# Two weight sums on VectorE, state additions ahead of the recombination, and the last product in banks of its own, in a fused attention and gated feed-forward kernel

## The chip, the cores and the metric

One core of one Trainium2 chip. The metric is the device time of the whole program in microseconds (us). The kernel before was given with a median of 321.29 us (three runs, 321.08 to 322.13). The span of the profiled execution is about 1.7 us shorter than the time of the same run, so spans and times are not mixed below.

## The reference, cut to what matters

```python
# q, k, v: (8 batches, 8 heads, 576 positions, 64); w_in (512, 2048); w_out (2048, 512)
scores = q @ k^T / 8                      # per batch and head
ret    = scores * Dmat                    # gamma_h ** (i - j) where i >= j, else 0
x      = (ret @ v) as (4608 tokens, 512)
h      = x @ w_in
out    = (h * cos(h)) @ w_out             # (4608, 512), float32
```

## The kernel before

The tokens go in ten blocks `n` of 512, 256, 256 and seven times 512. TensorE does all products. In each block it first multiplies by `w_in` (the rows `PE ... h<-xT,w_in_sb` of the profile), ScalarE takes the cosine, VectorE makes the gated activations `gT`, and then TensorE multiplies by `w_out`. Attention for later blocks (scores, states, output: `sc`, `st`, `ov`) is laid between the products. GpSimd (POOL) prepares token groups of 128: it scales queries and keys and casts values (`qks`, `vb`) once their loads have landed.

From block 3 on (`S7 = 3`) the last multiplication is done in 2x2 quarters with seven products instead of eight. That needs sums of weight quarters (`w_sums`), once, and sums of activation quarters (`g_sum`, tiles `gs`; the prediction calls them operand sums), in every block. The seven products are then added to and subtracted from each other on VectorE to give the four output quarters; this is called the recombination. A product's matmuls add up in an accumulator (`ps`), which lies in one or more banks of the memory that TensorE writes to. Products are made in the order 3, 4, 5, 2, 1, 7, 6. Products 3 and 4 need weight sums 3 and 4, which overwrite quarters of `w_out_sb` in place, so they cannot be made before block 2 has read the weights.

```python
def w_sums(x, e0, e1):
    # ... a, b, op_ by x; for x in (3, 4) the result overwrites quarter a of w_out_sb
    (nc.gpsimd if x in (3, 4) else nc.vector).tensor_tensor(
        out=w_sum[x][:, e0:e1], in0=w_quarter(*a)[:, e0:e1], in1=w_quarter(*b)[:, e0:e1], op=op_)

def g_sum(n, x, e0, e1):
    # ...
    i = (nc.vector if x == 5 or (n, x) == (S7, 1) else nc.gpsimd).tensor_tensor(
        out=tiles["gs", n, x][:, e0:e1], in0=i0, in1=i1, op=op_)

def sums_after(n, i):                      # after w_in multiplication number i of block n
    if n == S7:
        if i == 0:
            w_sums(3, 0, E2)
            w_sums(4, 0, E2)
        if i == 6:
            g_sum(n, 5, 0, 4)
            g_sum(n, 2, 0, 4)
        elif i == 7:
            for x, e in ((5, 4), (2, 4), (1, 0), (7, 0), (6, 0)):
                g_sum(n, x, e, E2)
    elif i in (3, 7):
        for x in (5, 2, 1, 7, 6):
            g_sum(n, x, i - 3, i + 1)

def product(n, x):                         # 16 matmuls of 256 columns
    if x in (3, 4, 1, 7):
        ps = psum.tile([P, 2, N2], F32, tag={3: "n", 4: "st", 1: "n", 7: "st"}[x], name="o")
    # ... else it accumulates: 5 on 3, 2 on 4, 6 on 1
    for e in range(E2):
        for j in range(2):                 # two row blocks
            nc.tensor.matmul(ps[:, j], lhsT=lhs[:, e, j * P : (j + 1) * P], rhs=rhs[:, e, :], ...)

def mm2_seven(n, at):
    # ...
    for x in (3, 4, 5, 2, 1, 7, 6):
        if x in at:
            at[x](*[both] * (x == 5))      # attention work laid before product x
        # ...
        product(n, x)
        # x == 2: c21 = copy of the accumulator (ScalarE), then
        nc.vector.tensor_tensor(out=u22, in0=u22, in1=tiles["o", 4], op=ALU.subtract)
        # x == 1, 7, 6: additions into u11, u11, u22; each result is stored and feed() called,
        # which queues the preparation, transposes and loads of later token groups

def unit7(g, more=True, then=lambda: None):
    copy = states([g + 1, g + 2], "b")()   # state products, then the state additions (VectorE)
    then()
    attn_out([g, g + 1], "m", nc.scalar.copy)
    if more:
        scores2(g + 2)                     # banks "a" and "b"
    copy(nc.scalar.copy)
```

## Time and profile before

Three numbers matter: 15.2 us in which TensorE waits once for the weight sums; about 31 us for each later block, which TensorE fills to 98%; and the last block, where TensorE waits for GpSimd's sums.

The second part of the page shows the span in 40 slices of 8 us, each digit a busy share in tenths; PEclk is the granted clock of TensorE.

```profile
PE   8899999999993079999999999999999999999984
POOL 2760176545434899959995999599969944970793
PEclk9999999999998559999999999999999999999999
```

The hole in TensorE's row, the only one, is at 96 to 120 us, with the clock at half. GpSimd is not full before it. The table of TensorE's waits names what ended them (who waited, for whom: total us, how often, the longest):

```profile
PE o L441 <- POOL w_out_sb L374: 15.2, 1, 15.2
PE sc L181 <- DVE s L263: 2.4, 4, 0.7
PE o L441 <- POOL gs L396: 1.7, 4, 1.3
```

GpSimd's timeline shows why the sums were late (start, duration, engine, line, operation, number; in brackets the idle time before it and what ended that):

```profile
103.41 1.04 POOL L138 TENSOR_TENSOR qks<-fq,gq 128x512 bf16<-128x512 f32 x1 [4.28 <-DMA fq<-in_q_dram]
107.07 1.04 POOL L138 TENSOR_TENSOR qks<-fq,gq 128x512 bf16<-128x512 f32 x1 [0.61 <-DMA fq<-in_q_dram]
109.26 0.61 POOL L145 CAST vb<-fv 128x512 bf16<-128x512 f32 x1
109.83 8.06 POOL L374 TENSOR_TENSOR w_out_sb<-w_out_sb 128x2048 bf16<-128x2048 bf16 x2
117.84 12.28 POOL L396 TENSOR_TENSOR gs<-gT 128x1024 bf16<-128x1024 bf16 x4
```

The weight sums stand behind the preparation of token groups 16 and 17, which waits for loads, and the activation sums stand behind the weight sums. TensorE's timeline of the same stretch:

```profile
113.92 3.57 PE L441 MATMUL o<-w_out_sb,gT 128*128 128x256 bf16 x16 [15.20 <-POOL w_out_sb L374]
124.75 0.40 PE L181 MATMUL sc<-qkT 64*128 64x128 bf16 x8 [0.57 <-DVE s L263]
130.17 3.67 PE L441 MATMUL o<-ws,gs 128*128 128x256 bf16 x32
133.68 13.98 PE L321 MATMUL h<-xT,w_in_sb 128*128 128x512 bf16 x62
```

Product 3 runs 113.92 to 117.5 at half clock (3.57 us for 16 matmuls; 1.8 at full clock), products 7 and 6 are the row at 130.17, and block 4 begins at 133.68. The wait on `DVE s` is a score product that needs the bank of the state products back. In block 6 one sees the order that causes it:

```profile
219.34 0.58 ACT L483 COPY ot<-o 128x512 f32<-128x512 f32 x1 [1.16 <-DMA fk<-in_k_dram]
219.96 0.69 DVE L484 TENSOR_TENSOR ot<-ot,o 128x512 f32<-128x512 f32 x1 [1.06 <-ACT ot L483]
220.56 0.42 DVE L261 COPY s<-st 128x256 f32<-128x256 f32 x1
221.02 0.42 DVE L263 TENSOR_TENSOR s<-st,s 128x256 f32<-128x256 f32 x1
221.59 0.40 PE L181 MATMUL sc<-qkT 64*128 64x128 bf16 x8 [0.68 <-DVE s L263]
```

VectorE waits 1.06 us for a ScalarE copy in order to recombine, and only then makes the state additions for which TensorE waits. The end of the span:

```profile
297.83 17.16 POOL L396 TENSOR_TENSOR gs<-gT 128x1024 bf16<-128x1024 bf16 x8 [12.14 <-DVE gs L396]
315.05 1.05 PE L441 MATMUL o<-ws,gs 128*128 128x256 bf16 x8 [0.16 <-POOL gs L396]
316.13 0.69 DVE L492 TENSOR_TENSOR ot<-o,ot 128x512 f32<-128x512 f32 x1 [1.39 <-PE o L441]
```

GpSimd makes eight sums in a row to 315.0 us, and the last eight matmuls start when it ends. After the last addition (316.82) 3.2 us pass to the end of the span at 320.0.

### The profile page before, as it was taken

What the parts mean: (1) busy time and instruction counts of PE and PEld (TensorE: products, weight loads), DVE (VectorE), ACT (ScalarE), POOL (GpSimd) and SP (SyncE); (2) the same over time, 40 slices, a digit from 0 to 9 for tenths busy, and PEclk for the clock granted to TensorE, in tenths of its full rate; (3) what the DMA queues carried; (4) which work ended last, traced back from release to release, by engine and by line L of the source; (5) the groups of instructions that cost most, each with busy time, mean ns of one, the idle gap of its engine ahead of it and who ended that gap; (6) DMA issues with size and microseconds to landing.
All of it is one profiled execution on the core that took longest, in us unless ns stands there. A gap on an engine that the chain in (4) does not pass through costs nothing.

```text
span 320.0 us, 6597 instructions
## 1 busy us (share of the span) xinstructions
PE 292.7 (91%) x2724; PEld 200.7 (63%) x2745; DVE 200.1 (63%) x238; ACT 139.3 (44%) x176; POOL 222.8 (70%) x181
## 2 busy tenths in 40 slices
PE   8899999999993079999999999999999999999984
PEld 3578458575882057746874676477647754884563
DVE  5767745747687026378767784778387747835832
ACT  2666225333463004364346472645265536525610
POOL 2760176545434899959995999599969944970793
PEclk9999999999998559999999999999999999999999
DMA  8999999999999994999969953997670250021012
GB/s 213 209 211 206 199 236 221 183 219 239 177 195 213 236 209 113 195 219 206 226 156 244 196 127 66 201 228 168 135 163 2 68 131 2 0 87 46 2 58 73
DMA packets 154109, 50.23 MB, mean 157 GB/s; under 512 B 140768, under 2 KB 153056, under 8 KB 154080
## 3 DMA queue, kind: packets, MB, share of 16 engines
q1 hardware_dynamic: 149856, 45.63, 72.6%
q0 software_dynamic: 4224, 4.19, 7.9%
q8 instruction: 21, 0.34, 0.5%
q14 instruction: 8, 0.07, 0.1%
HBM read 36.70 MB, written 9.44 MB: 144 GB/s over the span
## 4 chain that ended last, share of the span: by engine, by line
PE 68%; POOL 8%; SPq 8%; DMA 8%; DVE 3%; issue 3%; ACT 1%; POOLq 1%
PE h L321 32%; PE o L441 22%; DMA fk<-in_k_dram 8%; SPq L113 6%; PE o L338 6%; POOL gs L396 5%; PE sc L181 3%; PE ov L294 2%; PE ov L281 2%; POOL w_out_sb L374 1%; POOL qks L139 1%; SPq L154 1%; ACT cosh L329 1%; PE st L240 1%; DVE s L263 1%
## 5 line engine op out<-in xcount | busy, mean ns | idle before, releaser
L396 POOL TENSOR_TENSOR gs<-gT 128x1024 bf16<-128x1024 bf16 (+1 forms) x52 | 115.3, 2254 | 34.3 <-DVE gs L396 34.3
L321 PE MATMUL h<-xT,w_in_sb 128*128 128x512 bf16 (+2 forms) x820 | 126.8, 313 | 0.8
L330 DVE TENSOR_TENSOR gT<-h,cosh 128x1024 bf16<-128x1024 f32 x72 | 88.1, 1224 | 46.5 <-ACT cosh L329 46.3
L329 ACT ACTIVATE cosh<-h,half_pi 128x1024 f32<-128x1024 f32 x72 | 80.2, 1113 | 73.5 <-PE h L321 73.5
L321 PEld LDWEIGHTS <-w_in_sb 128*128 128x128 bf16 x832 | 75.9, 98 | 49.0 <-issue 0.4
L138 POOL TENSOR_TENSOR qks<-fq,gq 128x512 bf16<-128x512 f32 x32 | 34.0, 1061 | 43.5 <-DMA fq<-in_q_dram 43.3
L441 PEld LDWEIGHTS <-gs 128*128 128x128 bf16 x560 | 53.5, 98 | 10.1 <-POOL gs L396 2.9
L190 DVE TENSOR_TENSOR ret<-sc,tri 128x1024 bf16<-128x1024 f32 x32 | 38.0, 1219 | 18.5 <-PE sc L181 18.3
L139 POOL TENSOR_TENSOR qks<-fk,gk 128x512 bf16<-128x512 f32 x35 | 37.0, 1059 | 10.3 <-DMA fk<-in_k_dram 9.6
L441 PE MATMUL o<-w_out_sb,gT 128*128 128x256 bf16 x224 | 28.0, 286 | 15.2 <-POOL w_out_sb L374 15.2
L441 PE MATMUL o<-ws,gs 128*128 128x256 bf16 x336 | 38.7, 273 | 0.5 <-POOL gs L396 0.5
L441 PEld LDWEIGHTS <-gT 128*128 128x128 bf16 x224 | 22.7, 102 | 20.3 <-issue 15.6
L338 PE MATMUL o<-w_out_sb,gT 128*128 128x512 bf16 x121 | 28.8, 380 | 0.4 <-issue 0.2
L441 PE MATMUL o<-w_out_sb,gs 128*128 128x256 bf16 x224 | 26.2, 273 | 1.3 <-POOL gs L396 1.3
L306 ACT CAST xT<-ov 128x1024 bf16<-128x1024 f32 (+1 forms) x18 | 16.5, 917 | 24.3 <-PE ov L294 24.2
L145 POOL CAST vb<-fv 128x512 bf16<-128x512 f32 x32 | 19.6, 613 | 2.9 <-DMA fv<-in_v_dram 2.5
L338 PEld LDWEIGHTS <-gT 128*128 128x128 bf16 x128 | 11.8, 98 | 12.6
L254 ACT CAST sb<-s 64x256 bf16<-64x256 f32 x40 | 16.1, 403 | 0.6
L181 PEld LDWEIGHTS <-qkT 64*128 64x128 bf16 x288 | 8.7, 96 | 9.1 <-issue 5.5
L181 PE MATMUL sc<-qkT 64*128 64x128 bf16 x256 | 11.7, 223 | 2.9 <-DVE s L263 2.4
L475 ACT COPY ot<-o 128x512 f32<-128x512 f32 x7 | 4.1, 585 | 21.4 <-PE o L441 21.4
L348 ACT COPY ot<-o 128x512 f32<-128x512 f32 x8 | 4.7, 589 | 17.1 <-PE o L338 17.0
(72 smaller groups left out, 192.2 us busy)
## 6 DMA issues: line engine op xcount, KB each, us to landing
out_dram<-ot SPq DMA_DIRECT2D x36, 256.0 KB, 2.9
fk<-in_k_dram SPq DMA_DIRECT2D x32, 256.0 KB, 5.0
fv<-in_v_dram SPq DMA_DIRECT2D x32, 256.0 KB, 5.1
fq<-in_q_dram SPq DMA_DIRECT2D x28, 256.0 KB, 4.2
w_in_sb<-in_moe_w_in_dram POOLq DMA_DIRECT2D x4, 512.0 KB, 8.6
w_out_sb<-in_moe_w_out_dram POOLq DMA_DIRECT2D x4, 512.0 KB, 15.8
fq<-in_q_dram SPq DMA_DIRECT2D x2, 512.0 KB, 4.4
fq<-in_q_dram SPq DMA_DIRECT2D x8, 128.0 KB, 4.8
```

The source lines that it names most:

```text
L113: i = nc.sync.dma_start(f[p0:p1], src[b, :, s0 : s0 + p1 - p0, :].rearrange("h s d -> s h d"))
L138: nc.gpsimd.tensor_tensor(out=qks[:, 0], in0=fq, in1=tq, op=ALU.mult)
L139: (nc.vector if g == 3 else nc.gpsimd).tensor_tensor(out=qks[:, 1], in0=fk, in1=tk, op=ALU.mult)
L145: nc.gpsimd.tensor_copy(vb, fv)
L181: nc.tensor.matmul(ps[:, he, hg, :], lhsT=qkT[d0 : d0 + D, HG + hg, :], rhs=qT[d0 : d0 + D, hg, :], start=True, stop=True,)
L190: nc.vector.tensor_tensor(out=ret.rearrange("p a b i -> p (a b) i"), in0=ps.rearrange("p a b i -> p (a b) i"), in1=mask.unsqueeze(1).to_br ...
L321: nc.tensor.matmul(ps[:, j, :], lhsT=w_in_sb[:, dg, (et + j) * P : (et + j + 1) * P], rhs=xT[:, dg, c0 : c0 + w], start=(dg == 0), stop=(d ...
L329: nc.scalar.activation(cosh, ps, ACTF.Sin, bias=half_pi, scale=1.0)
L330: nc.vector.tensor_mul(gT[:, et : et + m, c0 : c0 + w], ps, cosh)
L338: nc.tensor.matmul(ps, lhsT=gT[:, et, tsi * P : (tsi + 1) * P], rhs=w_out_sb[:, et, :], start=(et == 0), stop=(et == ET - 1),)
L396: i = (nc.vector if x == 5 or (n, x) == (S7, 1) else nc.gpsimd).tensor_tensor(out=tiles["gs", n, x][:, e0:e1], in0=i0, in1=i1, op=op_)
L441: nc.tensor.matmul(ps[:, j], lhsT=lhs[:, e, j * P : (j + 1) * P], rhs=rhs[:, e, :], start=(x in (3, 4, 1, 7) and e == j == 0), stop=(e == ...
```

## The change

Three intents. (1) Weight sums 3 and 4 go to VectorE, in four pieces of half a sum, one after each of the first four gating multiplies of block 3. (2) The recombination additions are no longer issued right after their product; they are kept in a list and issued at the next product, in `unit7` after the state additions. (3) In the last block activation sum 1 goes to VectorE, and products 1 and 6 get three accumulators in separate banks (row block 0, and two halves of row block 1), finished, added and stored one after the other.

```diff
-        (nc.gpsimd if x in (3, 4) else nc.vector).tensor_tensor(
+        nc.vector.tensor_tensor(                                   # w_sums
@@
-        i = (nc.vector if x == 5 or (n, x) == (S7, 1) else nc.gpsimd).tensor_tensor(
+        i = (nc.vector if x == 5 or (x == 1 and n in (S7, len(widths) - 1)) else nc.gpsimd).tensor_tensor(
@@ sums_after
-            if i == 0:
-                w_sums(3, 0, E2)
-                w_sums(4, 0, E2)
+            if i < 4:
+                w_sums(3 + i % 2, i // 2 * 4, i // 2 * 4 + 4)
@@ product (cut)
+        elif x == 1:
+            ps = psum.tile([P, N2], F32, tag="n", name="o")
+            pt = psum.tile([P, 2, 512], F32, tag="a", name="o")
+            tiles["o", x] = [ps] + [pt[:, k, : N2 // 2] for k in range(2)]
+        if x in (1, 6) and n == last:
+            parts = [(0, 0, N2), (1, 0, N2 // 2), (1, N2 // 2, N2)]
+        order = [(e, i) for e in range(E2) for i in range(len(parts))]
+        if len(parts) > 2:
+            order.sort(key=lambda u: u[1])
@@ mm2_seven (cut)
+        def flush():
+            while pend:
+                pend.pop(0)()
+        def add(out_, in0, in1, op_=ALU.add):
+            pend.append(lambda: nc.vector.tensor_tensor(out=out_, in0=in0, in1=in1, op=op_))
         for x in (3, 4, 5, 2, 1, 7, 6):
             if x in at:
-                at[x](*[both] * (x == 5))
+                at[x](flush)
+            else:
+                flush()
             # each recombination: nc.vector.tensor_tensor(...) -> add(...)
+            else:                                                   # last product of the last block
+                for (j, c0, c1), ps in zip(parts, tiles["o", 1]):
+                    add(u22[:, j, c0:c1], ps, u22[:, j, c0:c1])
+                    flush()
+                    nc.sync.dma_start(out[r0 : r0 + P, N2 + c0 : N2 + c1], u22[:, j, c0:c1])
@@ at (cut: keys 4, 2 and 7 of blocks 3 and 4 are changed in the same way)
-                    1: lambda: unit7(g + 2),
+                    1: lambda then: unit7(g + 2, True, then),
```

More of the change, by code (lines that the diff above doesn't have):

```diff
@@ L423, in sums_after @@
                 g_sum(n, x, i - 3, i + 1)
+    last = len(widths) - 1
     def product(n, x):
         gT = tiles["g", n]
-        if x in (3, 4, 1, 7):
+        parts = [(j, 0, N2) for j in range(2)]
+        if x in (3, 4, 7) or (x == 1 and n < last):
             ps = psum.tile([P, 2, N2], F32, tag={3: "n", 4: "st", 1: "n", 7: "st"}[x], name="o")
-            tiles["o", x] = ps
-        else:
-            ps = tiles["o", {5: 3, 2: 4, 6: 1}[x]]
+            tiles["o", x] = [ps[:, j] for j in range(2)]
+            tiles["all", x] = ps
+        elif x == 1:
[4 more added lines that the diff above has]
+            parts = [(0, 0, N2), (1, 0, N2 // 2), (1, N2 // 2, N2)]
+        dst = tiles["o", {5: 3, 2: 4, 6: 1}.get(x, x)]
         lhs = {3: gT[:, :E2, :256], 4: gT[:, E2:, 256:]}.get(x)
@@ L438, in product @@
             rhs = w_sum[x]
-        for e in range(E2):
-            for j in range(2):
-                nc.tensor.matmul(
-                    ps[:, j],
-                    lhsT=lhs[:, e, j * P : (j + 1) * P],
-                    rhs=rhs[:, e, :],
-                    start=(x in (3, 4, 1, 7) and e == j == 0),
-                    stop=(e == E2 - 1 and j == 1),
-                    skip_group_check=True,
-                )
+        order = [(e, i) for e in range(E2) for i in range(len(parts))]
+        if len(parts) > 2:
+            order.sort(key=lambda u: u[1])
+        for e, i in order:
+            j, c0, c1 = parts[i]
+            nc.tensor.matmul(
+                dst[i],
+                lhsT=lhs[:, e, j * P : (j + 1) * P],
+                rhs=rhs[:, e, c0:c1],
+                start=(x in (3, 4, 1, 7) and e == 0 and (i == 0 or len(parts) > 2)),
+                stop=(e == E2 - 1 and (i == len(parts) - 1 or len(parts) > 2)),
+                skip_group_check=True,
+            )
+        return parts
     def mm2_seven(n, at):
         s0 = starts[n] // P
+        pend = []
+        def flush():
[3 more added lines that the diff above has]
+            pend.append(lambda: nc.vector.tensor_tensor(out=out_, in0=in0, in1=in1, op=op_))
         def new(tag):
@@ L462, in store @@
             feed(s)
-        def both():
-            nc.vector.tensor_tensor(out=u22, in0=tiles["o", 4], in1=u22, op=ALU.add)
         for x in (3, 4, 5, 2, 1, 7, 6):
             if x in at:
-                at[x](*[both] * (x == 5))
-            elif x == 5:
-                both()
-            product(n, x)
+                at[x](flush)
+            else:
+                flush()
+            parts = product(n, x)
             if x == 3:
                 u22 = new("a")
-                nc.scalar.copy(u22, tiles["o", 3])
+                nc.scalar.copy(u22, tiles["all", 3])
+            elif x == 4:
+                add(u22, tiles["all", 4], u22)
             elif x == 5:
                 c12, u11 = new("c"), new("b")
-                nc.scalar.copy(c12, tiles["o", 3])
-                nc.vector.tensor_tensor(out=u11, in0=u22, in1=tiles["o", 3], op=ALU.subtract)
+                nc.scalar.copy(c12, tiles["all", 3])
+                add(u11, u22, tiles["all", 3], ALU.subtract)
                 store(c12, 0, 1, s0)
@@ L482, in mm2_seven @@
                 c21 = new("d")
-                nc.scalar.copy(c21, tiles["o", 4])
-                nc.vector.tensor_tensor(out=u22, in0=u22, in1=tiles["o", 4], op=ALU.subtract)
+                nc.scalar.copy(c21, tiles["all", 4])
+                add(u22, u22, tiles["all", 4], ALU.subtract)
                 store(c21, 1, 0, s0 + 1)
+            elif x == 1 and n < last:
+                add(u11, tiles["all", 1], u11)
             elif x == 1:
-                nc.vector.tensor_tensor(out=u11, in0=tiles["o", 1], in1=u11, op=ALU.add)
+                for (j, c0, c1), ps in zip(parts, tiles["o", 1]):
+                    add(u11[:, j, c0:c1], ps, u11[:, j, c0:c1])
             elif x == 7:
-                nc.vector.tensor_tensor(out=u11, in0=tiles["o", 7], in1=u11, op=ALU.add)
+                add(u11, tiles["all", 7], u11)
+                flush()
                 store(u11, 0, 0, s0 + 2)
-            elif x == 6:
-                nc.vector.tensor_tensor(out=u22, in0=tiles["o", 1], in1=u22, op=ALU.add)
+            elif n < last:
+                add(u22, tiles["all", 1], u22)
+                flush()
                 store(u22, 1, 1, s0 + 3)
+            else:
+                for (j, c0, c1), ps in zip(parts, tiles["o", 1]):
+                    add(u22[:, j, c0:c1], ps, u22[:, j, c0:c1])
+                    flush()
+                    r0 = starts[n] + 256 + j * P
+                    nc.sync.dma_start(out[r0 : r0 + P, N2 + c0 : N2 + c1], u22[:, j, c0:c1])
     loaded = prepared = transposed = 4
@@ L728 @@
                     at = {
-                        4: lambda: scores2(g),
-                        2: lambda: unit7(g),
-                        7: lambda: unit7(g + 2, n > 3),
+                        4: lambda then: (then(), scores2(g)),
+                        2: lambda then: unit7(g, True, then),
+                        7: lambda then: unit7(g + 2, n > 3, then),
                     }
```

## The prediction

> **What bounds it now.** TensorE is busy 292.7 of 320.0 us (busy table). Its waits (table of waits) are few: 15.2 us once, on GpSimd's weight sums; 2.4 us in four waits on VectorE state additions; 1.7 us on GpSimd's operand sums at the end. From block 4 on, blocks repeat every 31 us with TensorE 98% busy; GpSimd works 27.5 us of each (17.2 sums, 10.3 preparation), so it follows.
>
> **1. Weight sums to VectorE (main term).** In the timeline TensorE stops at 98.7 us and restarts at 113.9. GpSimd runs the two sums (4.05 us each) from 109.8 to 117.9, because in its order they follow the preparation of token groups that waited for loads (103.4, 107.1). VectorE needs four pieces of about 0.68 us (its 128x1024 bf16 sums measure that), placed between gating multiplies that leave 0.5 us gaps: it lags by about 1 us, TensorE loses perhaps 0.4 us, then products 3, 4, 5 start at about 99.
>
> But not all 15.2 us return. The GpSimd operand sums of this block still follow the same load-paced preparation (done 109.9). Product 2 needs two of 2.1 us: not before 114.1. TensorE, through products 3, 4, 5, the scores and attention work by about 108.3, waits about 6 us there. Product 7's sum ends at 118.2, product 6's at 122.3 (they ended at 126.1 and 130.1, just ahead of TensorE). The granted clock fell to 0.5 some 3.5 us into the old wait and recovered 4.4 us after it; "TensorE: Matmul & The Clock Gate" (What's actually happening) states about 3.4 us for both, and this trace roughly agrees. So a 6 us wait again makes product 2 take 3.6 instead of 1.8 us. I put product 6's end at 124.7; before, block 4 starts at 133.8. Gain: 9.1 us. Later blocks are paced by TensorE and keep it; loads and preparation have 1 to 2 us of slack left in block 4.
>
> **2. State additions first.** In the timeline the second score matmuls wait 0.57 to 0.68 us because the state addition stands behind a recombination that itself waits for a ScalarE copy. Ahead of it, all three waits in blocks 5 to 7 go: 1.8 us. The one in block 3 falls under the new wait. The postponed additions have spare time before their accumulators are needed.
>
> **3. The end.** In the last block GpSimd makes eight sums from 297.8 to 315.0 and TensorE waits for the last four. Two go to VectorE (0.7 us each): GpSimd ends at about 311, and TensorE, at 1.8 us a product from 301.3 with small waits, ends at about 314.2 rather than 316.1. The last product's first row block is added and stored while the rest multiplies; after it only a 128x128 addition (about 0.25 us by size, against 0.69) and a smaller store remain. "GPSIMD Engine Reference" (Specifications) says VectorE instructions with two SBUF inputs contend with GpSimd; one such sum measures 0.81 instead of 0.69 us under GpSimd work, so the cost is small. Gain: 2.7 us.
>
> **Sum.** 321.3 - 9.1 - 1.8 - 2.7 = 307.7 us; range 304 to 312. Faster by over 2%: 0.95; within 2%: 0.04; slower: 0.01.
>
> **Right if:** the wait on weight sums is gone; one new wait of 5 to 7 us stands before product 2 at about 108, on GpSimd operand sums, with the clock at 0.5 for a few us around 114; block 4 starts at 124 to 125; waits on state additions nearly vanish; TensorE ends about 2.5 us before the end of the span.
>
> **Wrong if:** GpSimd's preparation shifts with the loads (earlier: the wait shrinks, gain up to 14 us; later: the gain shrinks); loads for block 4 come too late once it starts 9 us earlier; VectorE's lag stalls the gating of block 3; or contention slows GpSimd's sums.

## The result, and the profile after

The changed kernel took 307.79 us (median of four runs, 307.64 to 308.00), against 321.19 for the one before in the same comparison. Ratios are the mean time of one kernel's fast runs over that of the other's of the same rounds, so not quite the ratio of the medians: 0.9578 here, 95% interval 0.9558 to 0.9598. All runs quoted are fast ones, except where it is said.

The busy page and the waits of TensorE after it:

```profile
PE   8999999999999938999999999999999999999995
PEclk9999999999999988999999999999999999999999
```

```profile
PE o L452 <- POOL gs L396: 6.4, 3, 4.9
PE sc L181 <- DVE gT L330: 0.8, 2, 0.4
PE h L321 <- DVE gT L330: 0.3, 1, 0.3
```

The waits on weight sums and on state additions are gone; a new one of 4.9 us, on GpSimd's activation sums, has come. The timeline of block 3, all engines:

```profile
92.82 1.43 DVE L374 TENSOR_TENSOR w_out_sb<-w_out_sb 128x1024 bf16<-128x1024 bf16 x1
93.72 1.44 POOL L139 TENSOR_TENSOR qks<-fk,gk 128x512 bf16<-128x512 f32 x1
...
108.08 1.04 POOL L138 TENSOR_TENSOR qks<-fq,gq 128x512 bf16<-128x512 f32 x1 [1.90 <-DMA fq<-in_q_dram]
110.67 12.23 POOL L396 TENSOR_TENSOR gs<-gT 128x1024 bf16<-128x1024 bf16 x4
112.84 1.87 PE L452 MATMUL o<-w_out_sb,gs 128*128 128x256 bf16 x8 [4.92 <-POOL gs L396]
114.91 1.71 PE L452 MATMUL o<-w_out_sb,gs 128*128 128x256 bf16 x8 [0.20 <-POOL gs L396]
122.95 1.92 PE L452 MATMUL o<-ws,gs 128*128 128x256 bf16 x16 [1.24 <-POOL gs L396]
124.71 5.56 PE L321 MATMUL h<-xT,w_in_sb 128*128 128x512 bf16 x24
```

The preparation of group 17 still waits for its load (108.08), the activation sums start after it (110.67), product 2 starts with their first piece (112.84), product 6 waits for their last (122.95), and block 4 starts at 124.71 instead of 133.68. In block 6 the order on VectorE is turned round, and the scores are one row of 16 without a wait:

```profile
209.58 0.42 DVE L261 COPY s<-st 128x256 f32<-128x256 f32 x1 [0.82 <-PE st L240]
210.04 0.42 DVE L263 TENSOR_TENSOR s<-st,s 128x256 f32<-128x256 f32 x1
210.36 0.64 PE L181 MATMUL sc<-qkT 64*128 64x128 bf16 x16
210.38 0.68 DVE L472 TENSOR_TENSOR ot<-ot,o 128x512 f32<-128x512 f32 x1
```

The end: GpSimd's last three sums, TensorE's last products, and the last stores.

```profile
293.33 6.66 POOL L396 TENSOR_TENSOR gs<-gT 128x1024 bf16<-128x1024 bf16 x3 [0.63 <-DVE gs L396]
296.77 5.44 PE L452 MATMUL o<-ws,gs 128*128 128x256 bf16 x64
301.81 1.60 SPq L523 DMA_DIRECT2D out_dram<-ot  x3
302.25 0.49 DVE L472 TENSOR_TENSOR ot<-o,ot 128x128 f32<-128x128 f32 x2 [0.47 <-PE o L452]
```

GpSimd ends at 299.99, and the last three products run without a gap to 302.21. The last addition ends at 302.74 and the span at 305.9: again 3.2 us.

With three marks in the trace (first matmul of block 4, first matmul of the last block, end of the span) the difference can be laid out, and the same marks serve for every experiment. A run can start late by 3 to 4 us: in some profiled executions the start of the first blocks is delayed, and block 3's multiplications then begin near 91 or 92 us instead of 88. Only the first column feels that, and not by the whole delay (e3 started 3.9 us late, but its block 4 only 0.6 us after that of the kernel before); the two lengths do not. Spans are printed to 0.1 us, so the last column is good to 0.05 us only.

| kernel | block 4 starts | block 4 to last block | last block to end |
|---|---|---|---|
| before | 133.68 | 153.78 | 32.54 |
| after | 124.71 | 151.02 | 30.17 |
| gain | 8.97 | 2.76 | 2.37 |
| e1 weight sums alone | 128.54 (started 4.1 late) | 153.80 | 32.46 |
| e2 state additions alone | 131.97 | 151.03 | 32.50 |
| e3 end alone | 134.24 (started 3.9 late) | 153.79 | 30.17 |
| e4 sum 1 to VectorE alone | 133.15 | 153.78 | 30.37 |
| e5 split alone | 134.82 (started 2.8 late) | 153.78 | 32.80 |
| e8 whole weight sums | 125.10 | 151.02 | 30.18 |
| e9 deferred preparation | 121.97 | 156.17 | 30.16 |
| e10 sum 2 to VectorE | 120.80 | 152.51 | 30.19 |
| e11 both and sum 7 | 118.89 | 154.51 | 30.20 |

### The profile page after: what moved, and what is told of

Its sections match the earlier page's. It is cut to its first block, busy times and chain, and to the rows that moved or that the text cites. A ratio compares the mean times of both kernels' runs of the same rounds, so it can differ in the third digit from the quotient of the medians.

```text
span 305.9 us, 6636 instructions
## 1 busy us (share of the span) xinstructions
PE 291.2 (95%) x2740; PEld 200.4 (66%) x2761; DVE 203.4 (66%) x248; ACT 139.3 (46%) x176; POOL 211.8 (69%) x177
## 4 chain that ended last, share of the span: by engine, by line
PE 66%; DMA 11%; SPq 9%; POOL 7%; issue 2%; DVE 1%; ACT 1%; POOLq 1%; DVEq 0%
PE h L321 30%; PE o L452 22%; DMA fq<-in_q_dram 6%; SPq L113 5%; PE o L338 5%; POOL gs L396 3%; DMA fk<-in_k_dram 3%; SPq L154 3%; PE ov L294 2%; PE sc L181 2%; DMA fv<-in_v_dram 2%; PE ov L281 2%; POOL qks L139 1%; ACT cosh L329 1%; POOL qks L138 1%
## 5 line engine op out<-in xcount | busy, mean ns | idle before, releaser
L396 POOL TENSOR_TENSOR gs<-gT 128x1024 bf16<-128x1024 bf16 (+1 forms) x50 | 111.4, 2262 | 30.4 <-DVE gs L396 30.4
L138 POOL TENSOR_TENSOR qks<-fq,gq 128x512 bf16<-128x512 f32 x32 | 34.7, 1084 | 45.1 <-DMA fq<-in_q_dram 43.3
L452 PEld LDWEIGHTS <-gs 128*128 128x128 bf16 x576 | 54.5, 99 | 15.3 <-POOL gs L396 7.6
L452 PE MATMUL o<-ws,gs 128*128 128x256 bf16 (+1 forms) x352 | 38.4, 268 | 1.2 <-POOL gs L396 1.2
L452 PE MATMUL o<-w_out_sb,gs 128*128 128x256 bf16 x224 | 27.8, 282 | 5.2 <-POOL gs L396 5.1
L472 DVE TENSOR_TENSOR ot<-o,ot 128x512 f32<-128x512 f32 (+2 forms) x32 | 19.7, 619 | 15.9 <-PE o L452 15.8
L452 PE MATMUL o<-w_out_sb,gT 128*128 128x256 bf16 x224 | 25.9, 273 | 0.0
L452 PEld LDWEIGHTS <-gT 128*128 128x128 bf16 x224 | 21.7, 98 | 4.0
L338 PEld LDWEIGHTS <-gT 128*128 128x128 bf16 x128 | 11.8, 98 | 12.6
L472 DVE TENSOR_TENSOR ot<-ot,o 128x512 f32<-128x512 f32 x14 | 9.6, 685 | 12.7 <-ACT ot L502 9.6
L396 DVE TENSOR_TENSOR gs<-gT 128x1024 bf16<-128x1024 bf16 (+1 forms) x17 | 12.9, 774 | 0.4
L348 ACT COPY ot<-o 128x512 f32<-128x512 f32 x8 | 4.7, 588 | 17.1 <-PE o L338 17.0
```

Source lines behind the costliest of these rows:

```text
L138: nc.gpsimd.tensor_tensor(out=qks[:, 0], in0=fq, in1=tq, op=ALU.mult)
L338: nc.tensor.matmul(ps, lhsT=gT[:, et, tsi * P : (tsi + 1) * P], rhs=w_out_sb[:, et, :], start=(et == 0), stop=(et == ET - 1),)
L396: i = (nc.vector if x == 5 or (x == 1 and n in (S7, len(widths) - 1)) else nc.gpsimd).tensor_tensor(out=tiles["gs", n, x][:, e0:e1], in0=i ...
L452: nc.tensor.matmul(dst[i], lhsT=lhs[:, e, j * P : (j + 1) * P], rhs=rhs[:, e, c0:c1], start=(x in (3, 4, 1, 7) and e == 0 and (i == 0 or l ...
L472: pend.append(lambda: nc.vector.tensor_tensor(out=out_, in0=in0, in1=in1, op=op_))
```

## The experiments

Theory: block 3 was held by the engine that made the weight sums, and what remains there is held by the activation sums that stand behind load-paced preparation on GpSimd; the state additions and the end are separate gains. Rivals: the parts need each other; the half clock after the wait was the real cost; the pieces of the sums matter and not the engine; VectorE's lateness or the loads as such pace block 3. Each comparison has five rounds beside the kernel before.

### e1, e2, e3: one part at a time

e1 keeps (1) and undoes (2) and (3); e2 keeps (2); e3 keeps (3). Undoing (2) makes every addition immediate except that after product 4, which was late before, too:

```diff
         def add(out_, in0, in1, op_=ALU.add):
             pend.append(lambda: ...)
+            if x != 4:
+                flush()
```

With all three undone, the instructions of every engine stand in the same order as before.

> The weight sums alone go to VectorE in four pieces; recombination order and last block as before. My theory: block 3 is paced by GpSimd after the change, so the gain is the whole 9.0 us that the full change showed up to the start of block 4 (133.7 to 124.7 us), because the other parts do nothing useful before that point: about 312.2 us, with one wait of about 5 us before product 2. Rival: the state additions are needed for part of that gain in block 3, then this gives 8 us or less (313 or more).

> The state additions lead the recombination, alone. Theory: each wait on a state addition (0.57 to 0.68 us, four of them) disappears and TensorE, which paces these blocks, passes it on; with the small score waits that the traces show in the same places, 2.8 us in blocks 4 to 8 plus 0.6 in block 3: about 318 us. Rival: only the reported waits count, 1.8 us or less: 319.4 or more.

> The end alone: one operand sum of the last block on VectorE and the last product in banks of its own. Theory: the end is separate from the rest, 2.4 us (from the start of the last block to the end of the span 32.5 us before, 30.2 after): about 318.8 us. If it were bound to the other two parts (blocks arriving in another phase), it would differ from 2.4 by more than 0.5.

Measured, beside 321.69 us for the kernel before: e1 313.18 (ratio 0.975, 0.9705 to 0.9796), e2 317.45 (0.9882, 0.9839 to 0.9926), e3 319.11 (0.9909, 0.9868 to 0.995). The scatter of the kernel before on this chip (320.62 to 323.95) makes these intervals wide; within them the three gains add up to that of the change (14.8 us by these ratios, 13.6 by that of the change). The marks in the traces are sharper. e2 shortens the blocks from 4 on by 2.75 us and leaves the end alone; e3 shortens the end by 2.37 and leaves the blocks alone; e1 does neither. So the second and third parts are separate, and each gives in the full change what it gives alone. e1's median came 1 us above the expected 312.2, which lies at the edge of its interval, and it is past the mark of its rival (313 or more), so the times do not decide between them. The trace does:

```profile
114.50 12.22 POOL L396 TENSOR_TENSOR gs<-gT 128x1024 bf16<-128x1024 bf16 x4
128.54 13.98 PE L321 MATMUL h<-xT,w_in_sb 128*128 128x512 bf16 x64
```

From GpSimd's first activation sum to the start of block 4 it is 14.04 us in e1, and the same 14.04 us in the change (110.67 to 124.71). The wait on a state addition is still there in block 3 of e1 (0.40 us), but the wait for GpSimd behind it takes it up. So block 3 gains nothing from the other two parts. The size of the first gain, 9 us, rests on the full change: e1's profiled execution started 4.1 us late and was the slowest of its six.

e2's block 3 was also 1.7 us shorter. Of this the score rows gave 0.74 (0.57 of it the vanished wait), and 0.88 came from products 3 and 4 and the scores between them, because the clock came back at 117.0 us instead of 119.3. That is luck of the run: in e4, which changes nothing in block 3, the clock came back at 117.9, and from product 3 to block 4 it took 19.08 us instead of 19.76.

### e8: the engine or the pieces

```diff
-            if i < 4:
-                w_sums(3 + i % 2, i // 2 * 4, i // 2 * 4 + 4)
+            if i == 0:
+                w_sums(3, 0, E2)
+                w_sums(4, 0, E2)
```

> The full change, but each weight sum is one VectorE instruction of 2048 elements, both right after the first gating multiply, as GpSimd had them. Theory: what matters is the engine, not the pieces: VectorE is about 2 us late in block 3 and TensorE loses 1 us or so in it, but TensorE then waits for GpSimd in any case, so the time stays within 0.4 us of the change (307.8). Rival: pieces between the multiplies are needed, and time rises by 1 to 2.5 us.

Measured: 308.03 us, ratio to before 0.9579, against 0.9578 for the change. Whole sums make TensorE wait 1.4 us for gating in block 3 (0.3 with pieces), and the later wait for GpSimd shrinks from 4.9 to 4.4 us; block 4 starts at 125.10. From GpSimd's first activation sum to block 4 it is 14.04 us once more (111.06 to 125.10). What counted is that VectorE makes the sums. The pieces are tidy, but their gain disappears in the wait behind them. One rival was not tested: the sums could have stayed on GpSimd, but ahead of the preparation in its order. In the kernel before GpSimd stood idle for 5.18 us before 92.99 and for 4.28 us before 103.41, and one sum takes 4.05 us; in the change VectorE began the first piece at 87.35. So it is not shown that another engine was needed, and not only another place in GpSimd's order.

### e4, e5: the two halves of the end

Both have the weight sums and the state additions of the kernel before, so they take e3 apart. e4 leaves the last product undivided; e5 leaves sum 1 of the last block on GpSimd.

```diff
-    last = len(widths) - 1          # e4
+    last = len(widths)
```

```diff
-... or (x == 1 and n in (S7, len(widths) - 1)) else nc.gpsimd)     # e5
+... or (x == 1 and n == S7) else nc.gpsimd)
```

> Of the end, only the operand sum of product 1 in the last block moves to VectorE; the last product is not split. Theory: the last products waited for GpSimd, and without two of its eight sums TensorE ends about 2 us earlier: gain 1.9 us, about 319.3 us. Rival: the split and the early store are what gains, then this gives under 0.7 us.

> Of the end, only the split of the last product; all operand sums stay on GpSimd as before. Theory: the last half of the last product still waits for the last GpSimd sum, and only the smaller last addition gains: 0.3 to 0.5 us, about 320.8 us. Rival: the row blocks stored early shorten the end by 1 us or more.

Measured beside 321.80: e4 319.97 (ratio 0.994, 0.9907 to 0.9972), e5 322.71 (1.0034, 0.9991 to 1.0077). The last block took 30.37 us in e4 and 32.80 in e5, against 32.54 before and 30.17 with both. So moving one sum gives 2.17 of the 2.37 us. The split alone gives nothing, even a little less, where 0.3 to 0.5 us was expected, and its trace says why:

```profile
298.98 17.16 POOL L396 TENSOR_TENSOR gs<-gT 128x1024 bf16<-128x1024 bf16 x8 [12.14 <-DVE gs L396]
316.19 1.50 PE L453 MATMUL o<-ws,gs 128*128 128x256 bf16 x20 [0.48 <-POOL gs L396]
```

Row block 0 first means that it already needs the second piece of GpSimd's last sum; 20 matmuls (1.50 us) then remain after GpSimd, where the undivided product had 8 left (1.05 us, shown above at 315.05). The smaller last addition saves 0.2 us after the last matmul, less than is lost there.

### e6, e7: the clock

e6 fills the old wait, e7 the new one, with idle matmuls whose results are not used, so that the clock does not fall.

```diff
+        if (n, x) == (S7, 3):                                     # e6, in product of the kernel before
+            warm(ps.rearrange("p j c -> p (j c)"), 68)
```

```diff
+            if (n, x) == (S7, 2):                                 # e7, in the changed kernel
+                warm(psum.tile([P, 512], F32, tag="m", name="idle"), 20)
```

> The kernel before, with 68 idle matmuls of 512 columns (0.216 us each at full clock, 14.7 us) in the accumulator of product 3 during the 15.2 us wait. They are overwritten by the product. Theory: the granted clock stays at 1.0 and products 3 and 4 take 1.8 us each; but GpSimd's last operand sum ends at 130.1 us all the same, so product 6 cannot begin before it: block 4 starts about 1.7 us earlier, 319.5 us. It says how much of the 9 us of the first part was the clock. Rival: the clock was worth most of it, 4 us or more.

> The changed kernel, with 20 idle matmuls of 512 columns (4.3 us) in a free bank during its 4.9 us wait before product 2. Theory: the clock stays at 1.0, product 2 is faster, but product 6 waits for GpSimd's last sum (122.9 us) and absorbs it: within 0.3 us of the change, 307.8. Rival: the half clock after the wait costs time that shows at the end: 1 to 2 us faster than the change.

Measured: e6 321.93 us (ratio 1.0012, 0.9979 to 1.0045), no gain, and not the 1.7 us expected. The clock was at 1.0 throughout, product 3 took 1.91 us instead of 3.57, and TensorE then waited for the second weight sum, which the expectation had forgotten:

```profile
114.88 1.91 PE L443 MATMUL o<-w_out_sb,gT 128*128 128x256 bf16 x16 [1.47 <-POOL w_out_sb L374]
118.89 1.91 PE L443 MATMUL o<-w_out_sb,gT 128*128 128x256 bf16 x16 [1.55 <-POOL w_out_sb L374]
```

GpSimd also began its weight sums 0.94 us later in that execution (110.77), and block 4 started at 133.75. From the start of these sums to block 4 it is 22.98 us, against 23.85 before: so in these two executions the clock was worth 0.9 us there, and the later start took it back. Why GpSimd started later was not shown. e7 took 308.16 us (0.9584, 0.955 to 0.9618), 0.4 us above the change where 0.3 was allowed: with the clock at 1.0, product 6 waits for GpSimd all the same.

```profile
125.43 1.92 PE L452 MATMUL o<-ws,gs 128*128 128x256 bf16 x16 [1.90 <-POOL gs L396]
```

From GpSimd's first activation sum (113.15) to block 4 (127.19) it is 14.04 us here too, as with the half clock. So the rival that the clock was the real cost (4 us or more of the gain) falls for both kernels.

### e9, e10, e11: is it GpSimd's order that is left?

e9 defers the preparation of group 17 behind block 3's activation sums. e10 makes block 3's sum 2 on VectorE. e11 does both, and makes sum 7 on VectorE, after the scores and before product 2.

```diff
-            while prepared < min(loaded, NG, 2 * s + 7, s + 11):      # e9, e11
+            while prepared < min(loaded, NG, 2 * s + 7, s + 11, 17):
```

```diff
-        i = (nc.vector if x == 5 or (x == 1 and n in (S7, len(widths) - 1)) else nc.gpsimd)   # e10
+        i = (nc.vector if x == 5 or (n == S7 and x in (1, 2)) or (x == 1 and n == len(widths) - 1) else nc.gpsimd)
```

```diff
-                for x, e in ((5, 4), (2, 4), (1, 0), (7, 0), (6, 0)):    # e11; (1, 2) above becomes (1, 2, 7)
+                for x, e in ((5, 4), (2, 4), (1, 0), (6, 0)):
@@ mm2_seven, before product(n, x)
+            if (n, x) == (S7, 2):
+                g_sum(n, 7, 0, E2)
```

> The changed kernel, with GpSimd's preparation of token group 17 put behind block 3's operand sums. Theory: these sums wait only because they stand behind that preparation, whose loads land at 108 us; now they start at about 106.2, product 2 waits under 1 us, the last sum ends near 118.5 and block 4 starts near 120.4 instead of 124.7. Preparation of five groups after it pushes block 4's sums back some 1 to 2 us. Expected 304 us, range 303 to 305.5. Rival: the block is held by the data (gating) or by the loads as such, then within 0.5 us of 307.8.

> The changed kernel, with block 3's operand sum for product 2 on VectorE (two pieces). Theory: product 2 no longer waits for GpSimd (it starts near 108), and the wait moves to product 7, whose sum ends near 114.8, and to product 6, whose sum ends near 118.8: block 4 starts near 120.7, expected 304 us. Rival: VectorE is too busy there, its lateness delays the scores, and half or more of the 4 us is lost.

> Both remedies, and block 3's operand sum for product 7 on VectorE too, after the scores; GpSimd keeps only that of product 6. Theory: TensorE goes through block 3 with no wait over 1 us, the clock stays at 1.0, and block 4 starts near 117 us instead of 124.7. Then loads and preparation for block 4 are the next limit and may give back 1 to 2 us: expected 301 us, range 299.5 to 303.5. If the loads are what really paces it, little better than the single remedies: 304.

Measured beside 321.66: e9 310.04 us (0.9635, 0.961 to 0.966), slower than the change; e10 305.39 (0.9495, 0.9481 to 0.9509), faster; e11 306.87 (0.9533, 0.9507 to 0.9559).

In block 3 e9 and e10 do what the theory says, and e11 in part. Block 4 starts 2.7, 3.9 and 5.8 us earlier than in the change (in e9 about 1.6 us less than expected: a cast of GpSimd's waited 1.5 us until TensorE had read its buffer, and the sums began at 107.9). In e11 it starts at 118.9 us and not near 117, because with more sums on VectorE that engine's lateness, one of the rivals, becomes a limit. TensorE waits 1.67 us for it (0.82 in the same place in e10), where no wait over 1 us was expected:

```profile
108.36 0.32 PE L240 MATMUL st<-v_odd,qks 128*64 128x64 bf16 x8 [1.67 <-DVE ret L190]
```

In e10 product 2 follows the scores without a wait, and the waits after it in block 3 are those of products 7 and 6:

```profile
115.03 1.92 PE L452 MATMUL o<-ws,gs 128*128 128x256 bf16 x16 [1.02 <-POOL gs L396]
119.05 1.92 PE L452 MATMUL o<-ws,gs 128*128 128x256 bf16 x16 [2.09 <-POOL gs L396]
...
148.85 0.40 PE L181 MATMUL sc<-qkT 64*128 64x128 bf16 x8 [0.82 <-DMA qkT<-qks]
```

But the next block gives part back, by a wait that the change does not have: scores of block 4 wait for the transposes of token groups (`DMA qkT<-qks`), 1.25 us in e10. In e9 and e11 it is more. e9:

```profile
145.48 0.40 PE L181 MATMUL sc<-qkT 64*128 64x128 bf16 x8 [0.49 <-DMA qkT<-qks]
151.96 0.40 PE L181 MATMUL sc<-qkT 64*128 64x128 bf16 x8 [1.22 <-DMA qkT<-qks]
152.88 0.40 PE L181 MATMUL sc<-qkT 64*128 64x128 bf16 x8 [0.52 <-DMA qkT<-qks]
153.21 5.30 PE L452 MATMUL o<-ws,gs 128*128 128x256 bf16 x32
```

e9's block 4 lasted 36.4 us against 31.2 in the change: 2.2 us in these waits, 0.8 in one on VectorE, and 1.6 us because the last two products ran at half clock (5.30 us against 3.67). The times agree: e9's one run with a mean clock of 0.998 took 308.24 us, the others, with 0.986 to 0.994, 309.9 to 310.6. Its preparation of five groups after the sums ended at 134.0 us, and the sync queue issued group 17's transpose at 122.2 us instead of 112.6, with the loads that come after it in that queue. e11's block 4 lasted 34.7 us, 3.5 more, of which 2.7 are such waits. So the theory of block 3 holds, and the expected 304 us of e9 and e10 and 301 us of e11 failed on the next limit, the supply of prepared and transposed groups (in e11 also on VectorE). e11's interval touches that of the change (0.9558 to 0.9598), so it is not clearly faster.

e10 is better than both kernels: 305.39 us. It did not run on the chip of the change; against the kernel before, the ratios are 0.9495 (to 0.9509) and 0.9578 (from 0.9558), and the intervals do not meet.

### e12: what paces block 4 then

e12 is e11 without four output stores just before block 3 (wrong: those rows are missing).

```diff
-            nc.sync.dma_start(out[s * P : (s + 1) * P, :], ot)
+            if s < 4:
+                nc.sync.dma_start(out[s * P : (s + 1) * P, :], ot)
```

> The kernel with both remedies, and on purpose without the four output stores of block 1 and 2's rows 512 to 1023 (256 KB each; those rows of the result are missing, so it is wrong by intent). Its block 4 lasted 34.7 us instead of the change's 31.2, with waits on transposes and GpSimd waiting for loads. Theory: the sync queue and the transfers it issues pace that block; with 1 MB and four queue entries less just before it (about 4.7 us at 220 GB/s), preparation is done earlier and block 5 starts 3 us or more earlier than 153.6: about 302.5 us. Rival: GpSimd's own work or VectorE's lateness paces it, then block 5 starts within 1 us of 153.6 and the time stays at 305 to 307.

Measured: the fast runs lie between 303.77 and 306.15 us, ratio to before 0.9487 (0.9454 to 0.952), against 0.9533 (0.9507 to 0.9559) for e11. The profiled execution fell in the slow group (308.52 us) and its block lengths are not used. Four of the five fast runs lie above 305.3 us, where the rival had put them (305 to 307). This is inconclusive: the difference is 0.5% with overlapping intervals, less than the 4 us that the theory asked for. That block 4 of e11 waits for transposes is shown; which part of their supply is the tight one (the order in the sync queue, the bytes, or preparation behind late loads) stays open.

## Why the prediction was right

The time was 307.79 us for 307.7 predicted, and the range held it. Point by point:

- **Weight sums (9.1 us predicted, 8.97 measured).** Right, also in its main step, that not all 15.2 us return, because the activation sums stand behind load-paced preparation: a 4.9 us wait appeared before product 2, product 6 waited for the last sum (122.9 us, 122.3 predicted), and block 4 started at 124.71 (124.7 predicted). e9 and e10 confirm that step from two sides. Two details were wrong and cancelled. GpSimd started 0.8 us later than assumed. And product 2 did not need both pieces of its sum: its first eight matmuls started with the first piece, at 112.84 and not 114.1, which is why the wait was 4.9 us and not the 5 to 7 that the prediction asked for. Behind it product 6 needed 1.8 us after the last sum (122.9 to 124.71), where the prediction left 2.4, and that made up for the sum's 0.6 us.
- **The clock.** The prediction let the half clock lengthen product 2 to 3.6 us; its two halves took 1.87 and 1.71. e7 shows that this cost nothing, as the sum for product 6 came later still. "TensorE: Matmul & The Clock Gate" (What's actually happening) states that about 3.4 us of idling halve the clock and about 3.4 us of work restore it. In steps of 0.25 us, the clock fell 3.5 us after TensorE's last matmul in the kernel before and 5.0 us after it in the changed one, and came back 5.3 and 3.5 us after work resumed. The trace agrees with the page for one of each pair; the prediction had read 4.4 us for the recovery before, which is too short.
- **State additions (1.8 predicted, 2.76 measured).** The mechanism was right, the size too small. The three reported waits (0.57, 0.68, 0.57) are 1.82 us. The rest are delays in the same places which the table of waits does not list: about 0.17 us more in each of blocks 5 to 7, and in block 4 two rows of 16 score matmuls of 0.83 and 0.86 us that became 0.62 and 0.64. e2 alone gives the same 2.75.
- **The end (2.7 predicted, 2.37 measured).** The term for GpSimd was right: e4 gives 2.17 for about 1.9 predicted. The term for the early and smaller store, the other 0.8 us, was mis-sized: with the split it is 0.1 to 0.2 us more (30.37 to 30.17, each good to 0.05), and the split alone loses about 0.26. The prediction that TensorE ends 2.5 us before the end of the span was wrong: it ends 3.7 before (302.21 to 305.9), and from the last addition to the end it is 3.2 us as before, although the last stores landed 1.6 us after issue instead of 2.2 (medians). Three stores stood in one queue, and the last went out at 303.0, 0.3 us after the last addition; before, the last store went out at 316.85, 0.03 us after its addition.
- **VectorE's room.** "GPSIMD Engine Reference" (Specifications) says that VectorE instructions with two SBUF inputs contend with GpSimd for SBUF. The trace agrees: one piece of the weight sums took 1.43 us instead of 0.68 beside GpSimd's preparation, which took 1.44 instead of 1.04 (the rows at 92.82 and 93.72). TensorE's reported wait on the gating is 0.3 us, but block 3's multiplications by `w_in` took 11.4 us (87.97 to 99.35) instead of 10.65, so 0.7 us was lost and not the 0.4 predicted. It fell into the wait anyway.

The errors of size (-0.1, +1.0 and -0.3 us) cancel in part, and the profiled execution before was 0.4 us slower than the median from which the prediction was counted, so the closeness of the total is partly luck.

## What to carry to other kernels

When a wait is taken away, follow the engine that ended it: its later instructions are the next wait, and their place in that engine's order is what the gain is limited by. "GPSIMD Engine Reference" (Engine selection) advises VectorE for elementwise work with two inputs; here 128x2048 bf16 took 4.05 us on GpSimd and 1.22 on VectorE, so the few sums that TensorE is waiting for are worth VectorE's time (e1, e4, e10), while cutting them finely, keeping the clock up in a wait that another engine sets, or splitting the last store gave nothing that showed in the time (e8, e6, e7, e5). A remedy that only puts work off in an engine's queue can move the wait to the next block (e9).

## What the Trainium skill lacked or had wrong

- "TensorE: Matmul & The Clock Gate" (What's actually happening) says that the transition varies by about 500 ns, with where in a free-running window the first matmul lands. Here the fall came 3.5 and 5.0 us after the last matmul and the recovery 5.3 and 3.5 us after the first one, a spread of 1.5 to 1.8 us, in two kernels at the same stage. The clock records of the traces fit free-running windows of the length that the page gives, 3413 ns: the stretches at half clock lasted 17.07 us in the kernel before and 3.41 in the changed one, and 3.41, 6.83, 10.24, 13.65 or 17.07 us in the experiments (the last one of a trace, cut by its end, left out).
- The same section gives the half clock after at least one idle window of about 3.4 us. In e9 the clock fell at 153.2 us although TensorE's two pauses were 1.2 and 0.5 us and it was busy for 1.7 of the 3.4 us before, and it stayed at half for 3.4 us. A later section of the page (A second HAM failure mode: psum-queue depth-cycling) tells of falls from frequent short idles, but gives no figure for them. e11's times fall into two groups, 305.1 to 305.3 us with a mean granted clock of 0.998 or more and 306.9 to 307.2 with 0.992 to 0.994; whether it is the same effect was not shown.
- "GPSIMD Engine Reference" (Engine selection) gives about a factor of two for two-input elementwise work and names no type. For bf16 the trace shows 3.3 (4.05 against 1.22 us, 128x2048); no float32 pair was run here.
